# Rests of the feed-forward weights: prepared per tile in stage two, or in blocks of four tiles in stage one

## The chip, the core and the metric

The kernel runs on one core of a Trainium2 chip. The core has a matrix engine (TensorE, PE in the profile; its weight loads are PEld), a vector engine (VectorE, DVE), a scalar engine (ScalarE, ACT), a general-purpose engine (GpSimd, POOL) and a sequencer (SyncE, SP) that here issues the transfers between device memory (DRAM) and the on-chip memory SBUF. Sixteen DMA engines carry these transfers. Matmul results lie in eight PSUM banks. The metric is the device time of one execution in microseconds (us), as a median over runs.

## The reference, cut to what matters

A sequence of 2048 rows with 576 features goes through a memory-augmented attention `a` (32 heads, four segments of 512 rows) and a SwiGLU feed-forward `b` with 4608 inner features; a sigmoid gate mixes them.

```
def _B_ref(x, w_gate, w_up, w_down):
    g = _silu(x @ w_gate)          # 2048 x 576 by 576 x 4608
    u = x @ w_up
    return (g * u) @ w_down

g = _sigmoid((x * gate_w).sum(-1, keepdims=True))
a = _A_ref(x, A_wq, A_wk, A_wv, A_wo, A_beta)
b = _B_ref(x, B_w_gate, B_w_up, B_w_down)
return g * a + (1 - g) * b
```

The change touches only how `x @ w_gate` and `x @ w_up` are fed. All inputs are float32.

## The kernel before

**Two terms for a float32 value.** A float32 operand is split in two: `hi` is its rounding to the matmul's type (an ACT copy, L112) and `lo` the remainder (a DVE subtraction, L113). A product then takes three matmuls: hi by hi, hi by lo, lo by hi.

**Stage one** (0 to about 221 us) makes q, k, v and the memory term. It runs over four segments `s`. Each has nine "chains" `n` = 0 to 8 (function `qk`; 14 matmuls of 512 columns, L135) and then eight v steps (`v_step`; 14 matmuls of 288 columns, and evictions at L362 to L369 that ACT, DVE and POOL hand to one another); from segment 1 on every v step is followed by a `mem_step`. Work for later stages is put into this order by hand: functions in the list `mid` run inside a chain. Stores are gathered in `late`; `flush(2)` after a chain issues all but two, `flush()` ahead of a v step issues all. Among that work are the rests of x (`rest_load`, `rest_sum`, `rest_split`, the `xr` tiles), in segments 1 and 2, chains 2 and 4 to 8.

**Stage two** (about 221 to 1700 us) runs the feed-forward, with the attention in between. There are two halves: half 0 (to about 955 us) takes segments 2 and 3 of the rows, half 1 (to about 1700 us) segments 0 and 1. Each runs over 36 feature tiles `f` of 128 inner features. The product of (gate, up) by the two row segments is a 2 x 2 block product over two halves of the first 512 input features, and it is computed with seven products of sums instead of eight (`seven`, called seven times a tile). One product is six matmuls (L988, tiles `wo_` and `xo`) and one more, the rest matmul (L991, tiles `rh` and `xr`), for the last 64 of the 576 input features: its 128 rows are 32 rows of hi, the same hi again, 32 rows of lo, and 32 of zeros.

Three tiles `f` make a group; their down projection follows as "down groups" (L847, results added by DVE at L850 and L852). PE's order is laid down by `beat`, which takes down groups, attention steps (`att_gen`: scores L681 and L723, products with v L752 and L754) and deferred work in turn. `defer(k, fn)` puts work k beats ahead. The plan for the next tile is deferred at the start of the present one.

- In **half 0** the operands of tile f + 1 are made on chip by `w_make`: loads of the raw weights (L201), sums on POOL (L239), hi on ACT (L243), lo on DVE (L246), and a store of each operand to DRAM (`wc`, L256). The rests of the tile have a path of their own: `r_load` (L206; 256 KB, the 32 rows repeated three times, and zeros), four POOL sums of 128x128 (L211), one ACT copy of 128x896 (L250), one DVE subtraction of 32x896 (L253) and a store of 448 KB (`rc`, L259).
- In **half 1** `w_fetch` reads the seven operands of tile f + 1 (256 KB each, L653) and its rests (448 KB, L657) back. The rests are fetched in beat 1 of the plan and operand j in beat j + 2.

The engines' results of a product are taken out of PSUM by ACT (L1041 to L1060) and DVE (L1048, L1056, L1066). The attention's inputs are stacked by `stack_loads` (L172, issued at L789): ten transfers for each of 64 units, of which eight read with a leading dimension of 3 or 2; for the q side that dimension has step 0, so the same 18 rows are read 3 or 2 times:

```
qz = q[:, pr, z]
r += [(tq[r0:r0 + n * DH, pr],
       bass.AP(tensor=qz.tensor, offset=qz.offset, ap=[[0, n]] + list(qz.ap))),
      (tk[r0:r0 + n * DH, pr], k[:, pr, 0:n].rearrange("r z n -> z r n"))]
```

All these transfers are issued by SP, in the order of the program, and a transfer waits for the one eight places before it.

**The end** (to 1814 us) projects the attention's output, does the last down groups, and stores the result.

Of the kernel before, what the change touches and what calls it, by code (L numbers as in the profile page):

```python
# [12 lines left out]
F32 = mybir.dt.float32  # L13
# [44 lines left out]
def f32(ap):  # L58
    return ap.bitcast(F32)
# [3 lines left out]
def gated_mix(ctx, tc, xT, xrest, wf, wfr, wd, wv, wo, beta, cmask, ident, bmask, out):  # L63
# [75 lines left out]
    def x_slot(j, z, dtype=F32R):  # L139
        return xo.tile([P, 2, L], dtype, name=f"xo{j}{z}")  # L140

    def xr_tile(j):
        return xo.tile([P, L], F32R, name=f"xr{j}")

    def xs_split(xs, raw):
        nc.scalar.activation(xs, raw, AF.Copy)
# [54 lines left out]
        nc.sync.dma_start(r, wf[f][:, u, 0:4])  # L201
        return r

    def r_load(f):
        rraw_of[f] = rp.tile([P, 7, P], F32, name="rr", bufs=1)
        nc.sync.dma_start(rraw_of[f][:, 0:4], wfr[f])  # L206

    def r_total(f, j):
        r = rraw_of[f]
        o, p, q, sub = {4: (5, 0, 1, True), 1: (1, 1, 3, False), 2: (4, 1, 0, True), 5: (6, 2, 4, True)}[j]  # L210
        (nc.gpsimd.tensor_sub if sub else nc.gpsimd.tensor_add)(r[:, o], r[:, p], r[:, q])  # L211

    def r_totals(f, o):
        return [(o + n // 2, lambda j=j: r_total(f, j)) for n, j in enumerate((4, 1, 2, 5))]
# [7 lines left out]
    wraw_of, rraw_of, wops, wrem = {}, {}, {}, {}  # L222

    def op_tile():
        return wop.tile([P, 2, 2, P], F32R, name="wo_")

    def rem_tile():
        return wop.tile([P, 7, P], F32R, name="rh", bufs=2)

    def w_make(f):  # L230
        g, u = wraw_of.pop(f)
        ops, rem = [None] * 7, []
        wops[0, f], wrem[0, f] = ops, rem
        a11, a12, a21, a22 = g[:, 0:2], g[:, 2:4], u[:, 0:2], u[:, 2:4]
        src = [a11, None, None, a12, None, None, a22]

        def total(j, p, q, sub=True):
            src[j] = rp.tile([P, 2, P], F32, name="ws", bufs=3)
            (nc.gpsimd.tensor_sub if sub else nc.gpsimd.tensor_add)(src[j], p(), q())  # L239

        def high(j):
            ops[j] = op_tile()
            nc.scalar.activation(ops[j][:, 0], src[j], AF.Copy)  # L243

        def low(j):
            nc.vector.tensor_sub(ops[j][:, 1], src[j], f32(ops[j][:, 0]))  # L246

        def rem_high():
            rem.append(rem_tile())
            nc.scalar.activation(rem[0], rraw_of[f], AF.Copy)  # L250

        def rem_low():
            nc.vector.tensor_sub(rem[0][64:96], rraw_of.pop(f)[64:96], f32(rem[0][64:96]))  # L253

        def keep(j):
            nc.sync.dma_start(wc[f, j], f32(ops[j]).rearrange("p a k n -> p (a k n)"))  # L256

        def rem_keep():
            nc.sync.dma_start(rc[f], f32(rem[0]).rearrange("p j n -> p (j n)"))  # L259
# [20 lines left out]
    with ExitStack() as st:  # L280
# [255 lines left out]
                late.append((xrd[j], f32(XR[j])))  # L536

        XR = [None] * 7
        RSTEP = {4: (0, 3, -1), 5: (5, -4, 1), 6: (-2, 4), 7: (2, -6), 8: (6,)}
        FSUM = {4: [(1, 0), (4, 0)], 5: [(2, 0), (1, 1)], 7: [(4, 1), (2, 1)]}  # L540
        FSPLIT = {6: [(1, 0), (4, 0)], 7: [(2, 0), (1, 1)], 8: [(4, 1), (2, 1)]}
        for s in range(NSEG):
            upd = upd_gen(s - 1) if s else None
            casts = []
            for n, (m, u) in enumerate(chains):
                mid = []
                if s == 0:
                    for z in loads.get(n, []):
                        z()
                    if n + 3 < 9:  # L550
                        mid.append(lambda n=n: q_split(*chains[n + 3]))
# [9 lines left out]
                if 1 <= s < 3:  # L561
                    if n == 2:
                        rest_load(2 - s)
                    for j in RSTEP.get(n, ()):
                        mid.append(lambda j=j: rest_split(2 - s, j) if j >= 0 else rest_sum(-j))
# [12 lines left out]
                if upd is not None and n > 0:  # L578
                    next(upd, None)
            if s == 3:  # L580
                qst_.close()
                rp = pool(ctx, "rp", 4, side="right")
                wop = pool(ctx, "wop", 7, side="right")
                kq = pool(ast, "kq", 1, side="right")
                for i in range(NST):
                    if i < 2:
                        qst.append(kq.tile([P, 2, L], BF, name=f"qst{i}"))
                    if i < NST - 1:
                        kst.append(kq.tile([P, 2, L], BF, name=f"kst{i}"))
# [6 lines left out]
                r_load(0)  # L596
                start = w_make(0)
            for n in range(8):
                hf, i = divmod(n, 4)
                flush()  # L600
                v_step(s, hf, i)
                if s:
                    mem_step(s, n // 2, n % 2)
                if s < 3:
# [4 lines left out]
                else:  # L609
                    if n == 4:  # L610
                        wraw_of[1] = [w_load(1, u) for u in range(2)]
                    if n < 2:
                        first_sum(6, n)
                    elif n < 6:
                        if n - 2 < len(kst):
                            nc.gpsimd.memset(kst[n - 2], -1.0)
                    if n > 2:
# [5 lines left out]
        flush()  # L623
        while start[0][0] < 8:
            start.pop(0)[1]()
        r_load(1)
        for z in range(2):
            first_split(6, z)

# [1 line left out]
    with ExitStack() as st:  # L631
# [13 lines left out]
            return rw.tile([P, L], F32, name="row")  # L645

        def w_fetch(f):
            ops, rem = [None] * 7, []
            wops[1, f], wrem[1, f] = ops, rem

            def one(j):
                ops[j] = op_tile()
                nc.sync.dma_start(f32(ops[j]).rearrange("p a k n -> p (a k n)"), wc[f, j])  # L653

            def rest():
                rem.append(rem_tile())
                nc.sync.dma_start(f32(rem[0]).rearrange("p j n -> p (j n)"), rc[f])  # L657
# [294 lines left out]
        def x_second(new, rest):  # L952
# [43 lines left out]
        for pos, (half, f) in enumerate(seq):  # L996
# [184 lines left out]
```

## Time and profile before

| | us |
|---|---|
| median of three runs | 1823.78 |
| lowest and highest run | 1819.76, 1824.3 |
| the profiled execution | 1815.58 |
| its span, first to last instruction | 1813.9 |
| PE busy in it | 1786.2 |
| stage one, about | 0 to 221 |
| half 0, about | 221 to 955 |
| half 1, about | 955 to 1700 |
| three tiles in steady half 1 (from 1017.53 to 1084.41 in the chain of waits) | 66.9 |

The profile is one execution. A row of a timeline gives the start in us, the duration, the engine, the line of the kernel, the operation, the tiles written and read (`out<-in`), the shape, and a count where equal instructions are put together; in square brackets stands the idle time of the engine just before, and what ended it. A row of the waits gives the total idle time, how many times, and the longest. A row of the chain of waits gives start, duration and what the time went to; a DMA there lasts from its issue to its landing. A table by stretches gives the length of the stretch, for each engine its busy time (and its instructions), then the clock granted to PE (1.00 is full), the busy share of the DMA engines and the rate in GB/s. A busy PE is not PE at its peak: matmuls overlap, and slowed ones count as busy.

### The profile page before, as it was taken

The numbers are of one execution on the slowest core, as the hardware profiler recorded it, in microseconds if no ns is written. First come the engines' busy times: TensorE is split into PE (matmuls) and PEld (weight loads), VectorE is DVE, ScalarE is ACT, GpSimd is POOL, SyncE is SP. The second block draws the span as 40 slices with busy tenths as digits, with TensorE's granted clock in tenths as the row PEclk, the third lists the DMA queues.
The fourth block names the chain that finished last, engine by engine and source line by source line (L and its number), as shares of the span: only waits on it lengthen the run. The fifth ranks groups of instructions, "written<-read, shape, count | busy, mean of one in ns | idle before, by whom it ended". The sixth has DMA issues, their size and how long they took to land.

```text
span 1813.9 us, 36468 instructions
## 1 busy us (share of the span) xinstructions
PE 1786.2 (98%) x12445; PEld 1525.4 (84%) x12445; DVE 1321.0 (73%) x3263; ACT 979.5 (54%) x1805; POOL 896.9 (49%) x1143
## 2 busy tenths in 40 slices
PE   9999999999999999999989999999999999999999
PEld 7899878788888888888877888888888888888899
DVE  6656666788888888888877777777767777765455
ACT  7766564466556655665556455455455455354411
POOL 3434742446655665556545555555555555544121
PEclk9999999999999999999999999999999999999999
DMA  6555485676557755775577455455465455455644
GB/s 236 193 180 182 162 299 193 208 258 243 179 193 258 259 170 200 256 252 185 187 252 258 138 188 190 157 172 185 132 196 184 150 176 178 140 172 186 201 142 138
DMA packets 204329, 354.94 MB, mean 196 GB/s; under 512 B 41904, under 2 KB 79664, under 8 KB 204144
## 3 DMA queue, kind: packets, MB, share of 16 engines
q1 hardware_dynamic: 204144, 352.62, 57.7%
q8 instruction: 99, 1.62, 0.4%
q14 instruction: 86, 0.70, 0.1%
HBM read 209.54 MB, written 143.00 MB: 194 GB/s over the span
## 4 chain that ended last, share of the span: by engine, by line
PE 87%; DVE 4%; DMA 4%; issue 2%; ACT 2%; POOL 1%; SPq 0%; DVEq 0%; ACTq 0%; POOLq 0%
PE bank L988 32%; PE bank L847 24%; PE bank L135 12%; PE bank L991 5%; PE bank L723 4%; PE bank L681 4%; PE bank L752 2%; PE bank L754 1%; DMA rr<-in_wfr_dram 1%; PE bank L387 1%; DVE xo L113 1%; PE bank L433 1%; POOL rr L211 0%; DVE rh L253 0%; DVE bank L1048 0%
## 5 line engine op out<-in xcount | busy, mean ns | idle before, releaser
L847 PE MATMUL bank<-dw,hh 128*128 128x320 f32 (+1 forms) x2304 | 487.3, 304 | 6.0 <-DVE ya L852 4.0
L817 POOL TENSOR_TENSOR p<-pe,p 128x512 f16<-128x512 f32 x320 | 381.7, 1193 | 169.8 <-DVE p L815 97.1
L847 PEld LDWEIGHTS bank<-dw,hh 128*128 128x128 f32 x2304 | 377.1, 189 | 27.3 <-DVE ya L852 9.6
L727 ACT ACTIVATE pe<-bank 128x512 f32<-128x512 f32 x320 | 190.0, 594 | 305.4 <-PE bank L723 281.0
L847 PE MATMUL bank<-dw,hl 128*128 128x320 f32 (+1 forms) x1152 | 340.2, 295 | 0.3 <-DVE hl L113 0.3
L735 POOL TENSOR_SCALAR_AFFINE_SELECT pe<-pe 128x256 f32<-128x256 f32 (+1 forms) x320 | 136.0, 425 | 289.5 <-ACT pe L727 287.6
L688 DVE CUSTOM_DVE_ANT_0 scr<-bank,cm 128x512 bf16<-128x512 f32 (+3 forms) x512 | 247.7, 484 | 20.6 <-PE bank L681 12.5
L852 DVE TENSOR_TENSOR ya<-bank,ya 128x320 f32<-128x320 f32 x352 | 157.9, 453 | 115.2 <-PE bank L847 111.7
L847 PEld LDWEIGHTS bank<-dw,hl 128*128 128x128 f32 x1152 | 217.6, 189 | 0.9 <-DVE hl L113 0.9
L991 PE MATMUL bank<-xr,rh 128*128 128x512 f32 x504 | 197.4, 392 | 6.3 <-DVE rh L253 6.3
L723 PE MATMUL bank<-qst,kst 111*128 111x512 bf16 (+3 forms) x512 | 150.9, 303 | 0.0
L815 DVE CAST p<-pe 128x512 f16<-128x512 f32 x320 | 148.7, 465 | 0.0
L681 PE MATMUL bank<-kst,qst 108*128 108x512 bf16 (+3 forms) x512 | 126.0, 300 | 1.1 <-DVE mb L688 0.5
L211 POOL TENSOR_TENSOR rr<-rr 128x128 f32<-128x128 f32 x144 | 79.1, 549 | 83.6 <-DMA rr<-in_wfr_dram 68.1
L991 PEld LDWEIGHTS bank<-xr,rh 128*128 128x128 f32 x504 | 95.0, 189 | 27.5 <-issue 3.9
L931 DVE TENSOR_TENSOR hl<-row,hh 128x512 fp32r<-128x512 f32 x120 | 98.9, 824 | 24.8 <-ACT hh L930 24.8
L1051 ACT ACTIVATE row<-bank 128x512 f32<-128x512 f32 x72 | 43.0, 598 | 104.3 <-PE bank L991 104.3
L1055 ACT ACTIVATE bank<-bank 128x512 f32<-128x512 f32 x72 | 41.9, 582 | 105.8 <-PE bank L991 102.8
L1056 DVE TENSOR_TENSOR row<-bank,row 128x512 f32<-128x512 f32 x72 | 49.7, 691 | 66.5 <-ACT bank L1055 66.0
L239 POOL TENSOR_TENSOR ws<-raw 128x256 f32<-128x256 f32 x72 | 70.7, 982 | 55.0 <-DMA raw<-in_wf_dram 21.9
L1066 DVE TENSOR_TENSOR row<-bank,row 128x512 f32<-128x512 f32 x72 | 49.7, 690 | 60.3 <-PE bank L991 47.2
L135 PE MATMUL bank<-xo,qhi 128*128 128x512 f32 x288 | 91.3, 397 | 0.8 <-DVE xo L113 0.7
(1681 smaller groups left out, 4143.4 us busy)
## 6 DMA issues: line engine op xcount, KB each, us to landing
dc<-dw SPq DMA_DIRECT2D x36, 576.0 KB
dw<-dc SPq DMA_DIRECT2D x36, 576.0 KB
raw<-in_wf_dram SPq DMA_DIRECT2D x72, 256.0 KB
rc<-rh SPq DMA_DIRECT2D x36, 448.0 KB
rh<-rc SPq DMA_DIRECT2D x36, 448.0 KB
stk<-q SPq DMA_DIRECT2D x32, 384.0 KB
draw<-in_wd_dram SPq DMA_DIRECT2D x36, 288.0 KB
rr<-in_wfr_dram SPq DMA_DIRECT2D x36, 256.0 KB
```

The lines of the kernel that those rows point to most:

```text
L135: nc.tensor.matmul(t, st[n], mv[n], start=(n == 0), stop=(n == 13))
L681: nc.tensor.matmul(t[:, c:c + w], qs[:KR, pr, P * i:P * i + P], ks[:KR, pr, 0:w], start=True, stop=True)
L688: nc.vector.tensor_tensor_reduce(scr[:, :w], t[:, c:c + w], cm[:, L - w:L], 1.0, -3.0e38, OP.add, OP.max, m[:, k:k + 1])
L723: nc.tensor.matmul(t[:, c:c + w], ks[:KR + 3, pr, P * j:P * j + P], qs[:KR + 3, pr, P * j:L], start=True, stop=True)
L727: nc.scalar.activation(pe, t, AF.Exp, scale=SCALE)
L735: nc.gpsimd.affine_select(d, d, pattern=pat, compare_op=OP.is_ge, fill=0.0, base=0, channel_multiplier=-1)
L815: nc.vector.tensor_copy(p1, pe)
L817: nc.gpsimd.tensor_sub(p2, pe, p1)
L847: nc.tensor.matmul(t, p, q[:, cs], start=(n == 0), stop=(n == 3 * CH - 1))
L852: nc.vector.tensor_add(ya[:, i, cs], t, ya[:, i, cs])
L988: nc.tensor.matmul(t, w[:, p, z], x[z][:, q], start=first and n == 0, stop=False, skip_group_check=True)
L991: nc.tensor.matmul(t, rem[:, RPOS[j]], XR[j], start=False, stop=True, skip_group_check=True)
```

## The change

1. The rests of the weights are no longer loaded, summed, split and stored per tile in half 0 (`r_load`, `r_total`, `rem_high`, `rem_low`, `rem_keep` go). Instead nine blocks of four tiles each are made in stage one. The input array holds four tiles' 32 rows one below the other in 128 partitions, not one tile's rows repeated. A block `i` takes three steps: the load of the next block and four POOL sums (`b_sums`), the split of the four loaded arrays (512 columns), and the split of the three sums (384 columns). One step follows another in each chain from segment 0's chain 4 on and in each v step, until segment 1's v step 4. The two hi and two lo parts are stored to DRAM through `late`, 256 or 192 KB each. Staging uses the `xr` tiles, which are not needed until segment 2.
2. `rc` now keeps hi and lo apart, 32 rows a tile. Both halves fetch the rests of a tile by `r_fetch`: one transfer of 32 rows of hi into 64 partitions (read twice) and one of 32 rows of lo. It stands at beat 1 of the plan (10 for the first tile of half 1); tile 0's is issued in segment 3, v step 3. The two `rh` tiles are fixed, and their last 32 rows are set to zero once by POOL.
3. The rests of x move from segments 1 and 2 to segments 2 and 3, and the fetches of the second half's `xr` tiles come three beats earlier.

The number of matmuls stays the same.

```diff
-    rc = dram.tile([FT, P, 7 * P], F32, name="rc")
+    rc = dram.tile([2, 32 * FT, 7 * P], F32, name="rc")
...
-    def rem_tile():
-        return wop.tile([P, 7, P], F32R, name="rh", bufs=2)
+    def r_fetch(f):
+        for z, (a, n) in enumerate(((0, 2), (64, 1))):
+            src = rc[z, 32 * f:32 * f + 32]
+            nc.sync.dma_start(f32(rhs[f % 2][a:a + 32 * n]).rearrange("p j n -> p (j n)"),
+                              bass.AP(tensor=src.tensor, offset=src.offset, ap=[[0, n]] + list(src.ap)))
...
-        o = max(0, min(5, 6 - f))
-        if o > 1:
-            todo += r_totals(f, o - 2)
-        todo += [(o, rem_high), (o + 1, rem_low), (o + 2, rem_keep)]
-        if 0 < f < FT - 1:
-            todo.append((o + 2, lambda: r_load(f + 1)))
-            if f > 3:
-                todo += r_totals(f + 1, max(0, 5 - f) + 6)
...
+        def b_load(i):
+            rb[i] = xr_tile(6 * (i % 2), F32).rearrange("p (j n) -> p j n", n=P)
+            nc.sync.dma_start(rb[i], wfr[i])
+
+        def b_sums(i):
+            a, b = rb[i], xr_tile(1, F32).rearrange("p (j n) -> p j n", n=P)
+            rs[i] = b
+            nc.gpsimd.tensor_sub(b[:, 1], a[:, 0], a[:, 1])
+            nc.gpsimd.tensor_add(a[:, 1], a[:, 1], a[:, 3])
+            nc.gpsimd.tensor_sub(b[:, 0], a[:, 1], a[:, 0])
+            nc.gpsimd.tensor_sub(b[:, 2], a[:, 2], b[:, 0])
+
+        def b_split(i, z):
+            n = 4 - z
+            src = (rb, rs)[z].pop(i)[:, :n].rearrange("p j n -> p (j n)")
+            hi, lo = (xr_tile(k + z)[:, :P * n] for k in (2, 4))
+            split(hi, lo, src)
+            for k, t in enumerate((hi, lo)):
+                late.append((rc[k, P * i:P * i + P, 512 * z:512 * z + P * n], f32(t)))
...
+                if (s, n) == (0, 3):
+                    b_load(0)
+                if (s, n) > (0, 3) and blocks:
+                    mid.append(lambda z=blocks.pop(0): b_step(*z))
...
                 v_step(s, hf, i)
+                if blocks:
+                    b_step(*blocks.pop(0))
...
-            return [(j + 2 if f else FIRST[j], lambda j=j: one(j)) for j in range(7)] + [(1 if f else 10, rest)]
+            return [(j + 2 if f else FIRST[j], lambda j=j: one(j)) for j in range(7)]
...
-            todo += [(9 + j, lambda j=j: fetch(j)) for j in range(7)]
+            todo += [(6 + j, lambda j=j: fetch(j)) for j in range(7)]
...
+                plan.append((1 if nxt[1] else 10, lambda f=nxt[1]: r_fetch(f)))
...
-            ops, rem = wops.pop((half, f)), wrem.pop((half, f))[0]
+            ops, rem = wops.pop((half, f)), rhs[f % 2]
```

More of the change, by code (lines that the diff above doesn't have):

```diff
@@ L140, in x_slot, with xr_tile @@
         return xo.tile([P, 2, L], dtype, name=f"xo{j}{z}")
-    def xr_tile(j):
-        return xo.tile([P, L], F32R, name=f"xr{j}")
+    def xr_tile(j, dtype=F32R):
+        return xo.tile([P, L], dtype, name=f"xr{j}")
     def xs_split(xs, raw):
@@ L202, in w_load @@
         return r
[L204 to L214, printed above, removed]
     def d_load(f):
@@ L219, in d_load @@
         return r
-    wraw_of, rraw_of, wops, wrem = {}, {}, {}, {}
+    wraw_of, wops, rhs = {}, {}, []
     def op_tile():
         return wop.tile([P, 2, 2, P], F32R, name="wo_")
-    def rem_tile():
-        return wop.tile([P, 7, P], F32R, name="rh", bufs=2)
+    def r_fetch(f):
[3 more added lines that the diff above has]
+                              bass.AP(tensor=src.tensor, offset=src.offset, ap=[[0, n]] + list(src.ap)))
     def w_make(f):
         g, u = wraw_of.pop(f)
-        ops, rem = [None] * 7, []
-        wops[0, f], wrem[0, f] = ops, rem
+        ops = wops[0, f] = [None] * 7
         a11, a12, a21, a22 = g[:, 0:2], g[:, 2:4], u[:, 0:2], u[:, 2:4]
@@ L538, in gated_mix, with b_step @@
         XR = [None] * 7
-        RSTEP = {4: (0, 3, -1), 5: (5, -4, 1), 6: (-2, 4), 7: (2, -6), 8: (6,)}
+        RSTEP = {0: (0, 3, -1, 5), 1: (-4, 1, -2, 4), 2: (2, -6, 6)}
+        rb, rs = {}, {}
+        def b_load(i):
[15 more added lines that the diff above has]
+                late.append((rc[k, P * i:P * i + P, 512 * z:512 * z + P * n], f32(t)))
+        def b_step(i, k):
+            if k == 0:
+                if i + 1 < FT // 4:
+                    b_load(i + 1)
+                b_sums(i)
+            else:
+                b_split(i, k - 1)
+        blocks = [(i, k) for i in range(FT // 4) for k in range(3)]
         FSUM = {4: [(1, 0), (4, 0)], 5: [(2, 0), (1, 1)], 7: [(4, 1), (2, 1)]}
@@ L560, in gated_mix @@
                     mid.append(betas)
[L561 to L565, printed above, removed]
+                if (s, n) == (0, 3):
+                    b_load(0)
+                if (s, n) > (0, 3) and blocks:
+                    mid.append(lambda z=blocks.pop(0): b_step(*z))
+                if s > 1:
+                    if n == (2, 0)[s - 2]:
+                        rest_load(3 - s)
+                    for j in RSTEP.get(n - (4, 2)[s - 2], ()):
+                        mid.append(lambda j=j: rest_split(3 - s, j) if j >= 0 else rest_sum(-j))
                 if s == 3:
@@ L595, in gated_mix @@
                 wraw_of[0] = [w_load(0, u) for u in range(2)]
-                r_load(0)
+                for z in range(2):
+                    rhs.append(wop.tile([P, 7, P], F32R, name=f"rh{z}", bufs=1))
                 start = w_make(0)
@@ L614, in gated_mix @@
                     elif n < 6:
+                        if n < 4:
+                            nc.gpsimd.memset(f32(rhs[n - 2][96:]), 0.0)
+                        if n == 3:
+                            r_fetch(0)
                         if n - 2 < len(kst):
@@ L647, in w_fetch @@
         def w_fetch(f):
-            ops, rem = [None] * 7, []
-            wops[1, f], wrem[1, f] = ops, rem
+            ops = wops[1, f] = [None] * 7
             def one(j):
@@ L653, in one @@
                 nc.sync.dma_start(f32(ops[j]).rearrange("p a k n -> p (a k n)"), wc[f, j])
-            def rest():
-                rem.append(rem_tile())
-                nc.sync.dma_start(f32(rem[0]).rearrange("p j n -> p (j n)"), rc[f])
-            return [(j + 2 if f else FIRST[j], lambda j=j: one(j)) for j in range(7)] + [(1 if f else 10, rest)]
+            return [(j + 2 if f else FIRST[j], lambda j=j: one(j)) for j in range(7)]
         kp = pool(ast, "kp", 2, side="right")
```

11 lines of the change are left out of this document (1 added, 10 removed).

## The prediction, made before the changed kernel was run

> **What bounds the kernel now.** I read the page's busy table and costliest groups first.
>
> ```profile
> PE 1786.2 (98%) x12445; PEld 1525.4 (84%) x12445; DVE 1321.0 (73%) x3263; ACT 979.5 (54%) x1805; POOL 896.9 (49%) x1143
> ...
> L991 PE MATMUL bank<-xr,rh 128*128 128x512 f32 x504 | 197.4, 392 | 6.3 <-DVE rh L253 6.3
> ```
>
> TensorE (PE) is busy 1786.2 of 1813.9 us. A change that removes no matmul can win at most its 27.7 us of idle time and what slowed or spaced matmuls hide, while every new wait of PE costs its full length. Of the operations that the change takes out of half 0, only the split (L253) makes the rest matmul wait, 6.3 us in all. A table by stretches of the span shows where PE is idle:
>
> ```profile
> core 0: us, PE busy (x) PEld busy (x) DVE busy (x) ACT busy (x) POOL busy (x), PEclk, DMA share, GB/s
> 0.00:221.00 221.00, 218.01 (x1281) 193.27 (x1282) 138.40 (x317) 145.06 (x287) 102.62 (x117) 1.00 0.54 189
> 221.00:260.00 39.00, 32.63 (x131) 25.72 (x130) 26.08 (x48) 24.92 (x51) 13.88 (x23) 0.91 0.79 281
> 260.00:330.00 70.00, 66.23 (x354) 56.51 (x353) 49.27 (x106) 38.54 (x75) 25.38 (x37) 1.00 0.70 249
> 330.00:915.00 585.00, 583.38 (x3900) 498.36 (x3899) 488.11 (x1114) 344.95 (x665) 338.03 (x438) 1.00 0.62 215
> ...
> 985.00:1700.00 715.00, 713.50 (x5573) 595.45 (x5574) 505.01 (x1446) 358.92 (x606) 363.84 (x470) 1.00 0.53 168
> ```
>
> PE idles 6.4 and 3.8 us in the first two stretches of stage two, 3.0 in stage one (0 to 221) and 1.5 in half 1 (985 to 1700). That start is what the change can mend; the two long full stretches are what it can spoil.
>
> **Part 1, the rests leave half 0: a gain.** At the start PE waits for the rests' split, and once for work queued behind it (PE's timeline, then the others'):
>
> ```profile
> 226.65 0.77 PE L991 MATMUL bank<-xr,rh 128*128 128x512 f32 x1 [3.54 <-DVE rh L253]
> 227.21 2.76 PE L988 MATMUL bank<-xo,wo__2460 128*128 128x512 f32 x6
> 231.67 1.52 PE L988 MATMUL bank<-xo,wo__2578 128*128 128x512 f32 x6
> 242.25 0.50 PE L991 MATMUL bank<-xr,rh 128*128 128x512 f32 x1 [2.72 <-DVE rh L253]
> ...
> 314.40 1.00 POOL L211 TENSOR_TENSOR rr<-rr 128x128 f32<-128x128 f32 x2 [7.50 <-DMA rr<-in_wfr_dram]
> 318.07 1.25 DVE L253 TENSOR_TENSOR rh<-rr,rh 32x896 fp32r<-32x896 f32 x1 [0.28 <-ACT rh L250]
> 320.10 1.65 PE L988 MATMUL bank<-xo,wo__3528 128*128 128x512 f32 x6 [2.84 <-DVE bank L1048]
> ```
>
> 3.54 and 2.72 us are direct. The 2.84 us at 320.10 end the same chain: a load 7.50 us late, POOL's sums, the split to 319.32, and then L1048. All 9.1 us go. After the first wait six matmuls take 2.76 instead of 1.52 us. A granted clock of 0.91 over 39 us is 39 x 0.09 = 3.5 us, of which I count 3.0, since a part falls into the waits themselves. Late next is the first tile's own operand split on DVE, one such operation, 1.1 us. Gain 9.1 + 3.0 - 1.1 = 11; bounds 8 (the clock does not recover) and 13.
>
> From 330 to 915 PE is full, but its weight loads wait behind DVE:
>
> ```profile
> PEld bank L988 <- DVE bank L1048: 7.8, 18, 0.7
> ...
> 425.36 1.51 DVE L253 TENSOR_TENSOR rh<-rr,rh 32x896 fp32r<-32x896 f32 x1
> ```
>
> There the split of 1.51 us stands right ahead of L1048. The 18 waits of 0.43 us are partly covered by the matmul still in flight; at 0.3 us each 5.5 us come back; bounds 0 and 7.8. The loads, sums and copies that go besides are work PE does not wait for here.
>
> **Part 2, nine blocks in stage one: a loss.** Each block adds four POOL sums and two splits on ACT and DVE (512 and 384 columns), in 27 steps, one per chain or v step, from segment 0's chain 4 to segment 1's v step 4. The weak place is the v step:
>
> ```profile
> 43.45 0.46 ACT L368 ACTIVATE vps<-r 128x288 bf16<-128x288 f32 x1 [0.94 <-DVE r L363]
> 44.45 0.81 DVE L113 TENSOR_TENSOR xo<-xo,xo 128x512 fp32r<-128x512 f32 x1 [0.67 <-ACT xo L112]
> 45.66 0.46 ACT L368 ACTIVATE vps<-r 128x288 bf16<-128x288 f32 x1 [0.93 <-DVE r L363]
> 199.57 1.79 DVE L113 TENSOR_TENSOR xo<-qhi,xo 128x512 fp32r<-128x512 f32 x1
> ```
>
> ACT and DVE hand the v step back and forth, 45.66 - 43.45 = 2.21 us a turn, so work added to DVE lengthens the turn. A 512 split is 0.81 us on DVE, a 384 one three quarters, 0.61. Segment 0's eight v steps get two of the first and three of the second, 3.5 us, of which the spare PSUM banks hide about 1; segment 1's five get two and two, 2.8 us, of which 0.6 hide. Next to a POOL sum such a split has taken 1.79 instead of 0.81 us; I add 1 for that. Loss 2.5 + 2.2 + 1 = 5.7; bounds 0 (all hidden) and 3.5 + 2.8 + 2.7 = 9. In the chains DVE has room (138.4 of 221 us busy), so I count nothing there; without that room a split costs 0.8 us. The x rests, moved a segment later with the same operations, have the same cover and the same price. The rests' writes and loads in stage one find a DMA share of 0.54: nothing.
>
> **Part 3, the fetch: the term that decides.** The old fetch (L657) is 128 rows of 3.5 KB. The new one is two transfers: 32 rows read twice, by a leading dimension of 2 with step 0, into 64 partitions (224 KB), and 32 rows (112 KB). The first form stands in the kernel already: the stack loads (L789) lead with a dimension of 3 (54 KB) or 2 (36 KB). The DMA view from 1022 to 1027, where they run nearly alone (busy tenths of the 16 engines, and GB/s):
>
> ```profile
> DMA  0000000212212622221014516330000111001221
> GB/s 0 16 33 0 0 0 16 74 66 74 74 66 74 205 74 74 74 74 41 33 49 147 164 49 115 107 123 25 25 25 33 49 57 49 33 25 49 57 74 66
> ```
>
> With loads issued back to back the rate stands at 74 GB/s, and two tenths of the engines are busy. I read three engines for a leading 3 and two for a leading 2, at 74 / 3 = 24.7 GB/s each. So 224 KB (229 thousand bytes) on two engines are 114.7 / 24.7 = 4.6 us on each, 4.9 with the smaller transfer's 7.2 thousand; the old fetch on 16 is 28.7 / 24.7 = 1.2. What is queued behind it on those two engines is 3.7 us later, and every transfer over all 16 has a share there. The other bound is a fetch spread over 16 engines, 0.9 us: nothing lost. I take two engines, since the stack loads are the nearest rows.
>
> [...]
>
> In half 1 the transfers behind the fetch are the next tile's operands (L653) and the attention's stacks, which PE uses directly. The chain of waits shows how long such a transfer takes from issue to landing where PE waits today; the timeline, how soon after issue PE wants it:
>
> ```profile
> 979.18 6.42 DMA wo__12721<-wc
> 1327.47 5.75 DMA qst<-stk
> 1584.72 7.10 DMA wo__22260<-wc
> ...
> 961.77 0.36 SPq L653 DMA_DIRECT2D wo__12479<-wc  x1
> 969.49 0.47 PE L988 MATMUL bank<-xo,wo__12479 128*128 128x512 f32 x1
> ...
> 1706.19 0.58 SPq L653 DMA_DIRECT2D wo__23816<-wc  x1
> 1711.27 0.39 PE L988 MATMUL bank<-xo,wo__23816 128*128 128x512 f32 x1
> ```
>
> 5.75 to 7.10 us, say 6.3; with 3.7 more, 10. For each of the 36 old fetches (931 to 1701) I took the shortest time from issue to use among the operand and stack transfers issued in the 6 us behind it: 7.7 us behind the second (969.49 - 961.77), 5.1 behind the last, over 25 behind five. 19 are under 10 us, and what they lack adds up to 44 us: that much PE would wait. Against 9 us it is 28, against 11 it is 67. I take 44.
>
> In half 0 a load of 256 KB and a write of 448 KB (44 KB an engine) give way to the fetch (120 KB on two engines): 76 KB or 3.1 us more on those per tile. Operands are made on chip there, and the stacks are wanted 6.3 us after issue at the soonest, mostly after more than 8. I take 2 us; bounds 0 and 11 (half of its 22 stack sets 1 us late). The x rests' second fetch comes three beats earlier, in the stretch around 915 to 985: nothing, 2 us either way.
>
> **The sum**, against the profiled execution's 1815.6 us: -11 - 5.5 + 5.7 + 2 + 44 = +35.2, so 1850.8. That execution lies 8.2 us (0.45%) under the median of 1823.8; carried over, **1859**.
>
> **Rivals.**
> A, faster: the fetch spreads over all 16 engines. Its place is the queue behind the fetch, its price 0.9 us an engine instead of 4.9. Then -16.5 + 5.7 = -10.8 and 1813. Against it stand the 74 GB/s; for it, that the new rows are 3.5 KB and in 64 partitions, which no row shows. It decides from a lateness of 1.3 us downward: against 6.3 + 1.2 = 7.5 us the same tiles lack 8.6 us, which is what the rest of the sum gains (16.5 - 5.7 - 2 = 8.8).
> B, no change: two engines, but a PE that has waited issues the following transfers later too, so one wait serves several tiles and half 1 loses only a quarter, 11 us: 1823.8 + 11 + 2 + 5.7 - 16.5 = 1826. For it, several late tiles follow one another (958 to 987); against it, issue and use move together, so the next tile lacks the same time again.
> C, slower still: the two engines fill up. The DMA view of 1000 to 1690 has
>
> ```profile
> qst<-stk SPq DMA_DIRECT2D x76, 54.0 KB
> kst<-stk SPq DMA_DIRECT2D x76, 54.0 KB
> qst<-stk SPq DMA_DIRECT2D x114, 36.0 KB
> ```
>
> and as many of 36 KB for kst. At 18 KB on each of the two engines (4 KB for the third of the 36 KB loads that lead with 18 rows) that is 5.9 MB; the operands add 31 x 7 x 16.4 KB = 3.6 MB and the new fetches 31 x 122 KB = 3.8 MB: 13.3 MB or 540 of 690 us at 24.7 GB/s, 78% before the smaller transfers. Backlog would pass from tile to tile: the upper bounds of 67 and 11 us, 1823.8 - 16.5 + 5.7 + 78 = 1891.
>
> **How the numbers follow.** Forecast (two engines, half 1 loses 20 to 67 us): 0.68, its own range 1835 to 1882. A 0.13, B 0.09, C 0.10. Within 0.3% (5.5 us) a measurement of this kernel can't tell a change; two thirds of B lie there, the rest is slower: faster 0.13, same 0.06, slower 0.81. The range for 8 in 10 leaves out A and the far end of C: 1821 to 1893.
>
> **What would show it.** Right: in half 1 PE's waits name transfers (wo, qst, kst), tens of us in all, and its three-tile steps grow from 67 us to 70 or more, while half 0 keeps its pace; PE's waits of 3.5, 2.7 and 2.8 us at the start are gone; behind each fetch the DMA slices show one or two tenths. The forecast is wrong if half 1 stays as full as now (A), if stage one ends past 230 us, or if half 0 shows PE waiting for qst by more than 11 us.

## The result, and the profile after

| | before | after |
|---|---|---|
| median (four runs each, taken side by side) | 1821.77 us | 1973.76 us |
| lowest and highest run | 1818.33, 1824.3 | 1971.02, 1980.33 |
| span of the profiled execution | 1813.9 us | 1970.7 us |

The ratio is 1.0841, with a 95% interval of 1.0806 to 1.0876: 8.4% slower. Slower was forecast, but 1859 us, with 1893 as the upper end of its range.

The page of the changed kernel, its busy line and three of the costliest groups (line, engine, operation, tiles, shapes, count, then busy time and mean, then the idle time ahead and what ended most of it). The lines have moved: L999 is the rest matmul (L991 before), L996 the other product matmuls (L988), L689 the first score matmul (L681), L229 the sums of the raw weights (L239).

```profile
PE 1834.2 (93%) x12445; PEld 1549.3 (79%) x12445; DVE 1271.1 (64%) x3245; ACT 963.7 (49%) x1787; POOL 825.0 (42%) x1037
...
L999 PE MATMUL bank<-xr,rh 128*128 128x512 f32 x504 | 203.0, 403 | 36.1 <-DMA rh<-rc 36.1
L689 PE MATMUL bank<-kst,qst 108*128 108x512 bf16 (+3 forms) x512 | 128.1, 304 | 40.1 <-DMA kst<-stk 20.9
...
L229 POOL TENSOR_TENSOR ws<-raw 128x256 f32<-128x256 f32 x72 | 66.8, 928 | 179.4 <-DMA raw<-in_wf_dram 126.4
```

PE runs as many matmuls as before, 12445, but they take 1834.2 us instead of 1786.2, and it idles 136.5 us instead of 27.7. The waits are for transfers: in half 0 the rests themselves, in half 1 the stacks and the operands. POOL's sums wait 126.4 us for the raw weights, but this is POOL's idle time; what PE waits for in half 0 stands further below. DVE, ACT and POOL have less to do, as they should.

The table by stretches, with the halves cut at their first product; the changed kernel first, then the kernel before:

```profile
core 0: us, PE busy (x) PEld busy (x) DVE busy (x) ACT busy (x) POOL busy (x), PEclk, DMA share, GB/s
231.00:1013.00 782.00, 727.12 (x4620) 617.00 (x4620) 535.07 (x1290) 399.96 (x782) 300.72 (x371) 0.98 0.57 194
1013.00:1878.00 865.00, 797.01 (x5873) 650.96 (x5872) 531.09 (x1518) 396.37 (x663) 381.83 (x494) 0.96 0.49 151
```

```profile
221.50:956.00 734.50, 716.96 (x4623) 610.56 (x4623) 595.13 (x1328) 425.25 (x819) 393.42 (x511) 1.00 0.65 225
956.00:1721.00 765.00, 762.41 (x5871) 633.65 (x5870) 535.25 (x1518) 394.04 (x663) 381.93 (x493) 1.00 0.55 176
```

Stage one is 9.5 us longer, half 0 47.5 and half 1 100: 157 in all. Half 1's 100 us are 865 - 797 = 68 us of idle time instead of 2.6, and 35 us more busy time for the same matmuls, at a granted clock of 0.96 instead of 1.00. In half 0 PE idles 55 us instead of 18 and is busy 10 us longer.

One place in half 1, in the timeline of SP and then of PE:

```profile
1134.01 1.01 SPq L218 DMA_DIRECT2D rh<-rc  x2
1135.13 0.36 SPq L665 DMA_DIRECT2D wo__13869<-wc  x1
1135.59 0.38 SPq L790 DMA_DIRECT2D atd<-ob  x1
1136.02 1.11 SPq L190 DMA_DIRECT2D qst<-mxd  x1
1137.23 1.15 SPq L665 DMA_DIRECT2D wo__13903<-wc  x1
1138.55 0.39 SPq L665 DMA_DIRECT2D wo__13971<-wc  x1
1140.39 0.32 SPq L665 DMA_DIRECT2D wo__14001<-wc  x1
1145.03 0.32 SPq L665 DMA_DIRECT2D wo__14003<-wc  x1
```

```profile
1146.06 2.90 PE L996 MATMUL bank<-xo,wo__13869 128*128 128x512 f32 x6 [2.62 <-DMA wo__13869<-wc]
```

The chain of waits of the same stretch gives that operand's time from issue to landing:

```profile
1135.13 10.79 DMA wo__13869<-wc
```

Three things are to be seen. The operand issued right behind the fetch took 10.79 us; the prediction had set 10. SP then issued until the eighth transfer from the fetch's first (1140.39) and stood still for 4.3 us until the first, the large one, had landed; only then came the ninth (1145.03). The trace has this order throughout: 310 of SP's 313 waits for a transfer (those over 0.15 us) ended with the landing of the one eight places before, and 142 of 144 in the kernel before. And the six matmuls after PE's wait took 2.90 us instead of 1.52; the row for the 3 us from 1146 on has a granted clock of 0.53:

```profile
1146.00:1149.00 3.00, 2.94 (x7) 2.15 (x7) 0.00 (x0) 0.00 (x0) 0.00 (x0) 0.53 0.87 282
```

SP's waits from 1000 to 1850 (engine and line, what it waited for, total, times, longest) show the second in sum:

```profile
SPq L797 <- DMA rh<-rc: 54.2, 19, 4.3
...
SPq L665 <- DMA rh<-rc: 29.7, 9, 5.6
```

L797 are the stack loads, L665 the operands. In the kernel before SP's largest wait for a transfer in half 1 (985 to 1700) was

```profile
SPq L653 <- DMA kst<-stk: 13.4, 26, 0.8
```

All rows of SP's waits for transfers in half 1, added up, give 63 us before and 184 in the changed kernel.

Half 0 has the same, with another victim. Its chain of waits at one tile, and the DMA view around it (586 to 597; busy tenths of the 16 engines, GB/s):

```profile
586.60 9.66 DMA rh<-rc
596.25 0.14 issue
596.39 0.77 PE bank L999
597.16 2.43 PE bank L996 x6
```

```profile
DMA  5779999999999999999999799899742111111114
GB/s 103 195 263 359 399 399 428 418 432 414 398 412 367 412 389 397 400 400 395 438 395 350 231 216 298 315 382 367 276 179 76 48 56 48 56 50 45 52 52 171
```

At the end of the second view only the large transfer is left. The table by stretches has 52 GB/s for it from 594.8 to 596.3 us, at a DMA share of 0.13: 0.13 x 16 = 2.1, so two engines, at about 25 GB/s each. It lands 9.7 us after its issue, where tiles without attention follow one another in 11 to 12 us (427.66 to 438.97 in the kernel before), so its own rest matmul waits for it. PE's two large waits in half 0 (231 to 1013) are

```profile
PE bank L999 <- DMA rh<-rc: 36.1, 12, 8.1
PE bank L996 <- ACT bank L1050: 12.9, 16, 1.1
```

The second is ACT's eviction of a product. It stands behind other copies in ACT's order, and those wait for late transfers: one for a load of the down projection's weights (`draw`), another for the store of the earlier operand whose buffer it takes (`wc`), issued right behind the fetch. In the chain of waits, and in ACT's timeline:

```profile
384.42 5.38 DMA draw<-in_wd_dram
...
394.57 8.87 DMA wc<-wo__4352
```

```profile
403.52 0.42 ACT L233 ACTIVATE wo__4475<-ws 128x256 fp32r<-128x256 f32 x1 [4.01 <-DMA wc<-wo__4352]
```

Added up over half 0, that chain holds 70 us of the loads of the down projection's weights (`draw`, 12 pieces), 60 us of the rests (7) and 57 us of such stores (`wc`, 7). In experiment one, which has the change without the two-engine transfer, the same sums are 4, 0 and 16. The raw weights are in neither chain.

### The profile page after: what moved, and what is told of

Its sections match the earlier page's. It is cut to its first block, busy times and chain, and to the rows that moved or that the text cites. A ratio compares the mean times of both kernels' runs of the same rounds, so it can differ in the third digit from the quotient of the medians.

```text
span 1970.7 us, 36479 instructions
## 1 busy us (share of the span) xinstructions
PE 1834.2 (93%) x12445; PEld 1549.3 (79%) x12445; DVE 1271.1 (64%) x3245; ACT 963.7 (49%) x1787; POOL 825.0 (42%) x1037
## 4 chain that ended last, share of the span: by engine, by line
PE 58%; DMA 26%; DVE 6%; issue 3%; ACT 3%; SPq 2%; POOL 2%; DVEq 0%; ACTq 0%; POOLq 0%
PE bank L855 21%; PE bank L996 18%; PE bank L135 7%; DMA rh<-rc 6%; DMA draw<-in_wd_dram 4%; PE bank L999 3%; DMA qst<-stk 3%; PE bank L689 3%; DMA kst<-stk 3%; PE bank L731 3%; PE bank L760 2%; DMA qst<-mxd 1%; DVE xo L113 1%; PE bank L762 1%; DMA dw<-dc 1%
## 5 line engine op out<-in xcount | busy, mean ns | idle before, releaser
L999 PE MATMUL bank<-xr,rh 128*128 128x512 f32 x504 | 203.0, 403 | 36.1 <-DMA rh<-rc 36.1
L689 PE MATMUL bank<-kst,qst 108*128 108x512 bf16 (+3 forms) x512 | 128.1, 304 | 40.1 <-DMA kst<-stk 20.9
L999 PEld LDWEIGHTS bank<-xr,rh 128*128 128x128 f32 x504 | 98.3, 195 | 63.2 <-DMA rh<-rc 33.5
L229 POOL TENSOR_TENSOR ws<-raw 128x256 f32<-128x256 f32 x72 | 66.8, 928 | 179.4 <-DMA raw<-in_wf_dram 126.4
L689 PEld LDWEIGHTS <-qst 108*128 108x128 bf16 x512 | 50.6, 100 | 60.4 <-issue 35.1
```

The costliest lines, as they stand in the source:

```text
L689: nc.tensor.matmul(t[:, c:c + w], qs[:KR, pr, P * i:P * i + P], ks[:KR, pr, 0:w], start=True, stop=True)
L999: nc.tensor.matmul(t, rem[:, RPOS[j]], XR[j], start=False, stop=True, skip_group_check=True)
```

## The experiments

Each was timed beside the kernel before on the same chip (1820.7, 1820.25 and 1820.92 us in the three sets).

**One: the same bytes without the leading dimension of 2.**

```diff
-        for z, (a, n) in enumerate(((0, 2), (64, 1))):
-            src = rc[z, 32 * f:32 * f + 32]
-            nc.sync.dma_start(f32(rhs[f % 2][a:a + 32 * n]).rearrange("p j n -> p (j n)"),
-                              bass.AP(tensor=src.tensor, offset=src.offset, ap=[[0, n]] + list(src.ap)))
+        for z, a in ((0, 0), (0, 32), (1, 64)):
+            nc.sync.dma_start(f32(rhs[f % 2][a:a + 32]).rearrange("p j n -> p (j n)"),
+                              rc[z, 32 * f:32 * f + 32])
```

> The changed kernel with the hi rows fetched as two transfers of 32 rows each instead of one that reads them twice into 64 partitions; bytes, places in the order and everything else stay. Theory T (the leading dimension of 2 holds the large transfer to two DMA engines, and what is queued behind it is late): all three transfers run on 16 engines and land in about 3 to 5 us, the tiles are back at 60 us (half 0) and 67 us (half 1) per three, and the time is 1808 to 1828. Rival R (the two-engine form is not it; more and smaller transfers, the new layout of the stored rests or the blocks in stage one cost the time): stays above 1900, since none of these is undone and one transfer per tile is added.

1816.2 us (1811.76 to 1827.97), ratio 0.9984 (0.9965 to 1.0003). The loss is gone, with one transfer more per tile. T's time holds, R falls; on how many engines the three transfers ran, and when they landed, is not shown. In the changed kernel's trace, from 222.0 to 222.7 us, where the small transfer of 32 rows passes and little beside it, the DMA share is 0.61 at 177 GB/s. The halves of experiment one:

```profile
231.00:943.00 712.00, 706.12 (x4619) 609.81 (x4618) 528.04 (x1291) 396.25 (x782) 301.84 (x370) 1.00 0.63 213
943.00:1726.00 783.00, 769.75 (x5872) 637.13 (x5871) 534.28 (x1519) 395.27 (x662) 383.81 (x492) 0.99 0.56 167
```

The form of the one transfer is thus worth 782 - 712 = 70 us in half 0 and 865 - 783 = 82 in half 1. Half 0's 70 us are 36.1 + 12.9 = 49 us of the two waits above and 21 us of slower matmuls (727.1 against 706.1). Half 0 is now 22 us shorter than before. Half 1 is still 18 us longer than before (783 against 765), which T did not expect; experiments five and eight follow it. These are single executions, though: the profiled one here lies 5 us over its median (1821.25 against 1816.2), that of the kernel before 6 under (1815.58 against 1821.77), so up to 11 of the 18 us may be no more than that.

**Two: the two-engine form alone, in half 1 of the kernel before.**

```diff
-                nc.sync.dma_start(f32(rem[0]).rearrange("p j n -> p (j n)"), rc[f])
+                src = rc[f, 0:32]
+                nc.sync.dma_start(f32(rem[0][0:64]).rearrange("p j n -> p (j n)"),
+                                  bass.AP(tensor=src.tensor, offset=src.offset, ap=[[0, 2]] + list(src.ap)))
+                nc.sync.dma_start(f32(rem[0][64:]).rearrange("p j n -> p (j n)"), rc[f, 64:])
```

> The kernel before with one part of the change alone: in half 1 the first 64 rows of the rests are fetched by reading 32 rows twice (leading dimension 2, step 0), the other 64 rows by a second transfer. Stage one and half 0 stay as they were. T: half 0 keeps 60 us per three tiles, half 1 goes from 67 to about 75 us, as in the changed kernel; 1823 + 11 x 8 = about 1910 to 1925. R: within 10 us of before.

1935.65 us, ratio 1.0625 (1.0603 to 1.0647): 115 us, more than T's upper figure. The edit also makes one transfer a tile into two, which experiment eight prices at 12 us. Of the 121.5 us by which the span grows, 117 are in half 1:

```profile
960.00:1842.00 882.00, 800.63 (x5869) 651.26 (x5868) 530.42 (x1518) 396.17 (x662) 382.36 (x494) 0.96 0.51 153
```

81 us idle and 38 us of slower matmuls (800.6 against 762.4).

**Three: the two-engine form in half 0 only.** The changed kernel with the three transfers of experiment one in half 1.

> The changed kernel with the hi rows on 16 engines (two transfers of 32 rows) in half 1 only; half 0 keeps the transfer that reads them twice. T: half 1 back at 67 us per three tiles, half 0 stays at 64.5; the loss of half 1 (about 100 us) goes, the time is 1860 to 1885. R: above 1930.

1887.34 us, ratio 1.0364 (1.0349 to 1.038). Half 0 alone costs 71 us over experiment one, so it was no small matter. That is 2 us above T's range; half 1 still has its three transfers.

**Four: fetch two tiles ahead, in the same form.**

```diff
-                plan.append((1 if nxt[1] else 10, lambda f=nxt[1]: r_fetch(f)))
+                if pos + 2 < len(seq):
+                    plan.append((1, lambda f=seq[pos + 2][1]: r_fetch(f)))
```

with three tiles `rh` instead of two.

> The changed kernel with three tiles for the rests instead of two, and the fetch made two tiles ahead; its form stays (two engines). T (what counts is what stands behind the fetch): the waits for the rests themselves go (36 us of 47 with their slowed clock), but half 1 and the raw weights of half 0 stay late: 1915 to 1960. Rival L (what counts is that the fetch itself lands too late for its own tile): most of the loss goes, below 1880.

1993.54 us, ratio 1.0953 (1.0925 to 1.0982): slower still than the changed kernel, against both figures. PE's waits:

```profile
PE bank L996 <- ACT bank L1051: 61.9, 22, 9.2
PE bank L689 <- DMA kst<-stk: 17.3, 10, 3.5
```

The rests are no longer among the large ones. In their place PE waits for ACT, and ACT for the store of an earlier operand, as above. From ACT's timeline:

```profile
946.75 0.42 ACT L233 ACTIVATE wo__11110<-ws 128x256 fp32r<-128x256 f32 x1 [4.98 <-DMA wc<-wo__10987]
```

That store was issued right behind a fetch and took 8.8 us to land. POOL's wait for the raw weights grew as well, from 126.4 to 150.6 us, but the chain of waits of half 0 does not pass through these loads: it holds 109 us of such stores and 82 us of `draw`.

L falls: bringing the fetch earlier moves the wait to what is behind it. The waits for the rests went, as T said, but its time was too low, and the raw weights that it named are not what PE waits for. Why it is 20 us slower than the changed kernel was not followed further.

**Five: one transfer of 96 rows.** The hi rows are stored twice, and the input rows stand in the order row, tile instead of tile, row, so that a store leads with 32 and a tile's 96 rows lie together.

```diff
-    rc = dram.tile([2, 32 * FT, 7 * P], F32, name="rc")
+    rc = dram.tile([FT, 96, 7 * P], F32, name="rc")
...
+        nc.sync.dma_start(f32(rhs[f % 2][0:96]).rearrange("p j n -> p (j n)"), rc[f])
...
-            for k, t in enumerate((hi, lo)):
-                late.append((rc[k, P * i:P * i + P, 512 * z:512 * z + P * n], f32(t)))
+            for k, t in enumerate((hi, hi, lo)):
+                d = rc[4 * i:4 * i + 4, 32 * k:32 * k + 32, 512 * z:512 * z + P * n]
+                late.append((d.rearrange("t r n -> r t n"), f32(t)))
```

> The changed kernel with the rests stored so that a tile's 96 rows lie together (the hi rows are stored twice, 54 stores instead of 36; the input rows are ordered by row, then tile, so that stores and fetch lead with 32, 128 or 96), and fetched with one transfer of 96 rows. Theory P (in the version with three fetches on 16 engines, half 1 still takes 18 us more than before because three transfers a tile take more of SP's time and of its eight places): half 1 goes from 782 back to about 765 us, half 0 stays near 713, stage one near 231: about 1804 to 1812 against 1820 for before. Rival Q (that rest has another cause, such as half 1 starting at another point of the attention): half 1 stays above 775, the time at 1812 to 1820.

1807.68 us (1803.85 to 1808.99), ratio 0.9928 (0.9915 to 0.9941): 0.7% faster than before, and faster than experiment one. Its halves:

```profile
231.00:943.00 712.00, 705.56 (x4619) 610.18 (x4619) 527.53 (x1290) 396.41 (x782) 301.43 (x371) 1.00 0.62 213
943.00:1714.00 771.00, 763.50 (x5871) 633.71 (x5870) 534.44 (x1518) 394.24 (x662) 382.41 (x493) 1.00 0.56 170
```

Half 1 takes 771 us instead of 783, between P's 765 and Q's 775, and the time is P's. So P holds in the main. Of the profile's 12 us 8.5 stand in the medians (1816.2 against 1807.68). The 6 us that half 1 still lies over the kernel before are as much as that kernel's profiled execution lies under its median, so it is not shown that any loss is left.

**Six: blocks only within chains.** As five, with two steps a block, none in a v step.

> As the version with one transfer of 96 rows, but stage one makes the nine blocks only within chains (two steps a block, 18 chains, from segment 0's chain 4 to segment 2's chain 3), none in the v steps. If the v steps are where the blocks cost time, the first matmul of stage two starts at 223 to 227 us instead of 231, and the kernel is 4 to 8 us faster than the version with one transfer. If the blocks cost their time in the chains too, it starts at 231 or later, and nothing is gained.

1808.04 us, ratio 0.9931 (0.9917 to 0.9944): nothing gained. PE's longest wait in stage one:

```profile
47.09 3.22 PE L135 MATMUL bank<-vw,xo 128*128 128x288 f32 x12 [5.69 <-DVE vf L334]
```

The first product of stage two starts at 231.2 us, where it starts at 230.8 in five and at 221.5 before. PE waits for DVE's evictions in segment 0's v steps, now in one piece, although no block is worked on there. DVE's timeline just ahead has the reason:

```profile
44.92 0.69 DVE L113 TENSOR_TENSOR xr<-xr,xr 128x512 fp32r<-128x512 f32 x1 [4.51 <-DMA rc<-xr]
```

The split of a block that the chains had begun stands still for 4.5 us until an earlier block's store has left the staging tile, and the evictions queue behind it. With two steps a block instead of three the same staging tile is wanted again sooner. So six made a new wait and doesn't show what blocks in chains cost by themselves: set matmul against matmul, it has lost 8.3 of its 9.7 us by the end of segment 0's v steps, and nothing in the chains of segment 1.

**Seven: half the bytes.** The kernel before with one more transfer, half the size of the change's large one, into an unused buffer.

```diff
+                dum = rp.tile([P, 7, P], F32, name="rr", bufs=1).rearrange("p j n -> p (j n)")
+                src = rc[f, 0:32, 0:448]
+                nc.sync.dma_start(dum[0:64, 0:448],
+                                  bass.AP(tensor=src.tensor, offset=src.offset, ap=[[0, 2]] + list(src.ap)))
```

> The kernel before with one more transfer per tile in half 1, ahead of the fetch of the rests, into a buffer that is not used otherwise: 32 rows of 448 columns read twice into 64 partitions (112 KB, leading dimension 2, so 57 thousand bytes on each of two engines). Half of the bytes of the change's large transfer. Theory N (a wait is what the lateness exceeds the shortest time from issue to use by, so it grows faster than the bytes): lateness 2.3 us, shortfall against 8.6 us 22 us, half as much again for the slowed clock: 25 to 40 us over before. Rival proportional: the 115 us of the full transfer by 2.3 / 3.7, 60 to 75 us.

1869.74 us, ratio 1.0282 (1.0261 to 1.0304), 49 us over before: between the two. Alone it doesn't tell them apart. Experiment eight gives a price to a further transfer as such, 12 us each; with it N's 25 to 40 become 37 to 52, in which 49 lies, but that was put together afterwards.

**Eight: two more transfers of 32 rows.**

```diff
+                dum = rp.tile([P, 7, P], F32, name="rr", bufs=1).rearrange("p j n -> p (j n)")
+                for z in range(2):
+                    nc.sync.dma_start(dum[32 * z:32 * z + 32], rc[f, 32 * z:32 * z + 32])
```

> The kernel before with two more transfers per tile in half 1, ahead of the fetch of the rests, of 32 rows each (112 KB on 16 engines), into a buffer that is not used otherwise. P (more transfers cost by SP's time and its eight places): 10 to 20 us over before. Q: within 5 us, since 0.6 us an engine is all that they add.

1845.38 us, ratio 1.0132 (1.0117 to 1.0148): 25 us for what the expectation had estimated at 0.6 us an engine per tile (2 x 114.7 thousand bytes over 16 engines at 24.7 GB/s; that they spread over 16 was its assumption). Q is excluded; P holds, and was set too low. SP's waits for transfers in half 1 add up to 109 us instead of 63, which fits P; that the busier engines (0.59 instead of 0.55) have no part in it is not shown. PE's largest wait in half 1 is one that the kernel before does not have:

```profile
PE bank L684 <- DMA kst<-stk: 11.9, 9, 2.3
```

**Nine: no block step in segment 0's v steps.** As five, from chain 3 on, over a longer stretch.

> As the version with one transfer of 96 rows, but no block step in segment 0's v steps: 27 steps from segment 0's chain 3 on, in all chains and in segment 1's v steps, until segment 2's chain 3. In the version it starts from, stage one loses 5.1 of its 9.3 us in segment 0's v steps. If they are the weak place, the first matmul of stage two starts at 225 to 228 us instead of 231 and the time is 1802 to 1806. If the blocks only shift the loss to the next full place, it starts at 230 or later and the time stays at 1807 to 1810.

1803.69 us (1801.44 to 1804.94), ratio 0.9909 (0.9894 to 0.9925), the lowest median of the study. The first product of stage two starts at 228.1 us instead of 230.8, just past the first theory's range; the intervals of nine and five overlap a little. Neither theory is the whole of it. Set matmul against matmul, the kernel is 0.6 us behind the kernel before at the end of segment 0's v steps, where five is 3.0 behind (the 5.1 of the expectation is reached only at the start of segment 1's v steps). But it loses 3.4 us in segment 2's chains, which now hold the last blocks, where five loses 0.7 there. So most of what the v steps of segment 0 cost has shifted, and the gain comes from segment 1.

**Ten: the large transfer from GpSimd's queue.**

> The changed kernel with only the issue of the large transfer (32 rows read twice) moved from SP to GpSimd, which has a queue of its own and takes none of SP's eight places; the small one stays on SP. Theory P (most of the loss is SP standing still while the long transfers hold its places): at least two thirds of the 157 us over before go, below 1875. Theory E (most of it is the busy engines themselves, whoever issues): above 1920. [...]

1920.75 us, ratio 1.0543 (1.0519 to 1.0567): of the changed kernel's 152 us over before (in medians) 100 remain and a third goes. That is E's figure, if narrowly (1920 was its bound, and the median's interval holds it). The DMA view of the run has a queue (q0, 16.65 MB) that the pages of the kernel before and of the changed one do not have; the 72 large transfers of 229 thousand bytes make 16.5 MB. Their median of 10.1 us is near the 9.66 and the 11 that such a transfer took from SP in the places shown above, and GpSimd itself works on its issue (the DMA issues with the median from issue to landing, and the groups by line):

```profile
rh<-rc POOLq DMA_DIRECT2D x72, 224.0 KB, 10.1
```

```profile
L218 POOL DMA_DIRECT2D rh<-rc x72 | 49.5, 688 | 77.7 <-PE bank L999 41.3 <-issue 22.8 <-PE bank L996 10.5
```

Since GpSimd's own work and waits are new, how the loss divides between SP's places and the busy engines stays open. That more transfers in SP's queue cost time without a transfer that leads with 2 is shown by eight (25 us); that two thirds of the loss stay when SP is free of the large transfer, by ten, with GpSimd's own share in them unknown.

## Why the prediction was wrong in size

**The direction and the cause were right.** The deciding term was the fetch, and its form was read rightly from the stack loads: beside their 74 GB/s for a leading dimension of 3 there now stand 52 GB/s at a DMA share of 0.13 for one of 2: about 25 GB/s an engine, with the 74 read as three engines. Why a transfer of this form takes no more engines the traces don't show. Experiment one shows that the form is the cause: without it the loss is gone. Experiment two shows that it suffices, with one more short transfer beside it.

Against the forecast's +35 us the profiled span grew by 157. Half 0's term for the fetch was 68 us too low (2 against 70), half 1's 56 (44 against 100), stage one's loss 4 (5.7 against 9.5), and the gain was 6 larger than forecast (22.5 against 16.5): 68 + 56 + 4 - 6 = 122, which is the whole difference.

**The sizes of that term were wrong, in three steps.**

1. *"In half 0 ... I take 2 us; bounds 0 and 11"* is the step that failed most. Experiment one against the changed kernel gives 70 us, experiment three 71. Two paths stood at nothing. The fetch's own landing was never set against its own tile: it was priced for what stands behind it only. At 9.7 us in a tile of 11 to 12 it is late itself, 12 times, 36.1 us in all. And "operands are made on chip there" left out that their stores, and the loads of the down projection's weights, go by the same queue and engines: where one of them is late, a copy on ACT waits for it, and PE waits for the eviction behind that copy, 12.9 us. The other 21 us are slower matmuls.
2. *"That much PE would wait"*: the 44 us counted idle time only. In half 1 the idle time grew by 65 us (68 - 2.6), near the upper bound of 67; but the same matmuls were also 35 us slower after the waits. The row with 2.76 instead of 1.52 us stood in the prediction, and was used for the gain at the start and not for the loss.
3. *"What is queued behind it on those two engines is 3.7 us later"* took the engines' queue alone. SP's eight places hold more: it stood still for up to 5.6 us until the fetch had landed, and then everything behind it was issued late, operands of 256 KB too (1145.03 above). Experiment eight prices such a queue without a transfer that leads with 2, at 25 us; how much of the changed kernel's loss it makes up stays open, since ten, where the large transfer holds no place of SP's, wins back a third and adds costs of its own.

Rival C (1891) named the direction of the error, but with backlog on the engines as its mechanism and the same missing terms. Its 4 KB an engine for the loads that lead with 18 rows agrees with the kernel before: from 1024.66 to 1024.86 us, where such loads pass, the DMA share is 0.58, or 9.3 of 16 engines, and 36 KB / 9 = 4 KB. Rival B, in which half 1 loses only 11 us, is excluded by the 68 us.

Of the prediction's own signs, PE's waits in half 1 name transfers, as it said, and the waits for the split at the start are gone (the rests' first fetches there cost 8.1 and 2.9 us instead). But half 0 did not keep its pace (782 us instead of 734.5), and stage one ended past 230 us, which it had named as a sign of being wrong.

**The other terms, by experiment five**, which has the change without the form. Half 0: 734.5 - 712 = 22.5 us gained, against 16.5. Stage one: first product at 230.8 instead of 221.5, 9.3 us lost, against 5.7 and a bound of 9. Set matmul against matmul (the changed kernel against the kernel before, the last and first v matmuls of each segment), 3.1 us of these arise in segment 0's v steps and 3.0 in segment 1's, together about what the prediction had for the v steps (how much of the added work the spare PSUM banks would hide was its estimate). The rest is where it counted nothing: 2.0 us in segment 1's chains, and 1.3 later. Half 1: 6 us lost, against nothing, which may be the difference of two executions, as said. Together 22.5 - 9.3 - 6 = 7 us of profiled time and 12.6 us of median, where 10.8 stood for this case (rival A).

## What to carry to other kernels

Before a transfer is split or folded, write down its leading dimension, and look up in a trace what rate a transfer of that form gets: here a saving from 448 KB to 336 was lost many times over, since the new form ran at 52 GB/s. Price a slow transfer by three things, not one: what queues behind it on its engines (stores too, since they keep buffers: a store issued right behind a fetch took 8.87 us), how long it holds a place in its issuing queue (SP stood still for up to 5.6 us), and whether its own consumer still has the time (36.1 us of PE's waits in half 0). Before a long wait of one engine is called the cause, see whether the chain of waits passes through it. And where PE waits for microseconds, add what the matmuls lose after the wait; here, in half 1, it was 35 us beside 65 of waits.

## What the runs showed of the hardware that was not expected

- The matmuls after a wait of 2.62 us ran at about half speed (2.90 us for six instead of 1.52, at a granted clock of 0.53 over 3 us). In half 1 of the changed kernel, with waits of up to 5.2 us, the mean granted clock was 0.96 instead of 1.00, and 4% of 865 us are the 35 us by which its matmuls were slower.
- Two short transfers of 112 KB (32 rows), added to a tile of 22 us, cost 25 us over 36 tiles (experiment eight), though the DMA engines were only 0.55 to 0.59 busy.
- From GpSimd's queue the transfer of 64 rows took 10.1 us from issue to landing (median), and its 72 issues kept GpSimd busy for 49.5 us.
